# Moving one state product to another accumulator bank, and four steps of a hand-written schedule, in a fused state-space and feed-forward kernel

## The chip, the cores and the metric

The kernel runs on one NeuronCore of a Trainium2 chip. Five engines work side by side, each through its own queue in the order in which the program emits: TensorE (PE, with its weight loads shown as PEld), VectorE (DVE), ScalarE (ACT), GpSimd (POOL) and SyncE (SP), whose queue issues most DMAs here. The metric is the time of one execution on the device in microseconds. The kernel before takes 117.77 us, the median of six runs (117.53 to 119.92).

## The reference

Two stages follow each other. The first is a chunked state-space recurrence over batch 4, 8 heads, 768 positions, head size 32 and state size 16; the second is a feed-forward layer with a squared ReLU over 3072 rows, 256 wide, 2048 hidden:

```
for each chunk c of 32 positions:
    cum    = cumsum(log a)                       # in the chunk
    M      = (C B^T) * exp(cum_i - cum_j) * (i >= j)
    y      = M x + (C state) * exp(cum)
    state  = exp(sum log a) * state + sum_j B_j x_j exp(cum_last - cum_j)
x = y as rows of 3072 x 256
out = max(x w_in, 0)^2 w_out
```

The chunk length changes nothing in the result. The kernel uses longer stretches of its own.

## The kernel before

**Units and blocks.** The sequence is cut into 12 units, `UNITS[k] = (b, j)`: batch b and a third j of its positions, 256 rows, k = 4 j + b. A unit of the first stage becomes a block of 256 rows of the second. All is done in bf16 products with float32 accumulation.

**First stage of a unit k.** `ph_load` (line 124) brings B, C and x to the tiles `B_nat`, `C_nat`, `x_nat`. `prep_c` and `prep_b` (lines 161 and 169) multiply C and B with decay factors into `jt[k % 3]`, two instructions each; `prep_x` (line 180) casts x to `xs`. All three are POOL's from the third unit's C on, except some early ones. `ph_tr` (line 199) transposes jt to `bct`: for k < 5 with six PE transposes and a copy from PSUM by DVE (by ACT for k = 1), for later units with one DMA transpose on SP's queue. `ph_mt` (line 231) makes the scores, 16 products into four PSUM banks 0 to 3; `ph_mask` (line 253) multiplies one bank with the causal mask on DVE into `mts`, four times per unit. `ph_yu(y, u)` (line 260) makes the output products of unit y, first those from the incoming state (`from_state`, which read `Sd`), then, in the same call, the state products of unit u (`state_products`, two results U of 64 columns), then the products within the unit; ACT copies the outputs to `T`. `ph_s(k, i)` (line 333) turns U into the running state z (ACT's copy, or DVE's instruction of line 349) and then makes `Sd` on POOL (line 354), which the next output products read.

**Second stage.** For each of 8 steps f of a block: `mm1` (line 368), the up-projection, four 128x256 products into a PSUM bank, then ReLU by ACT to `hb`; `square` (line 380) on DVE; `mm2` (line 386), the down-projection, four products into bank 7 (bank 6 for block 0), which after the eighth step are copied by ACT and sent to memory by SP.

**Banks.** PSUM has 8 banks of 512 float32. 0 to 3 hold scores, 7 (or 6) the down-projection, and 4, 5 and 6 go round by `bank()`, least recently taken first; a bank that holds U is in `held` until `ph_s` has been emitted. `ph_s` reads U, so what overwrites that place waits for it.

**The order of the work.** It is written by hand; no planner moves anything. Blocks 0 and 1 follow the list `first` (line 539). From step 16 on, one up-projection is emitted in each step s, `ups[s]`; `at(s, fn, ...)` puts first-stage work ahead of it, in the order in which the `at` calls were made, then come the square of the step before and a down-projection. Step 22 has no down-projection; before it, `mm2(2, s - 19)`, after it, `mm2(*ups[s - 4])`. In step 19 the order for POOL is: `prep_x` of unit 4, then `Sd` of unit 3 twice (from `ph_s`), then `prep_c` and `prep_b` of unit 5. In SP's queue stand, in this order: the loads of units 3, 4 and 5, two output stores, the loads of unit 6, the transpose of unit 5, the loads of unit 7, the next store and the transpose of unit 6.

Of the kernel before, what the change touches and what calls it, by code (L numbers as in the profile page):

```python
# [16 lines left out]
def _fap(base: bass.AP, offset_elems: int, free_dims):  # L17

    ap0 = list(base.ap)[0]
    return bass.AP(tensor=base.tensor, offset=base.offset + offset_elems,  # L20
                   ap=[list(ap0)] + [list(d) for d in free_dims])
# [9 lines left out]
def kernel(  # L31
# [69 lines left out]
    held = set()  # L101

    def take(*hs):
        for h in hs:
            assert h not in held
            order.remove(h)
            order.append(h)

    def bank(edge=False):

        h = next(h for h in order if not (edge and h == 5))
        take(h)
        return h

    def two_banks():
        h = min(((4, 5), (5, 6)), key=lambda p: max(order.index(i) for i in p))
        take(*h)
        return h
# [80 lines left out]
    def ph_tr(k):  # L199
        v = live.setdefault(k, {})  # L200
        bct = big.tile([128, 2, 3, 128], BF16, tag="bct", name=f"bct{k}")
        v["bct"] = bct
        if k >= NPE:
            nc.sync.dma_start_transpose(out=bct.rearrange("p r w t -> p (r w) t"),
                                        in_=jt[k % 3].rearrange("p r w t -> p (r w t)"))
            return
        if k == 0:
            for r in range(2):
                tr = pp[:, 6 + r, 0:192].bitcast(BF16)
                for w in range(3):  # L210
                    nc.tensor.transpose(tr[:, w * 128:(w + 1) * 128], jt[0][:, r, w, :], eye_b)
                o = bct[:, r].rearrange("p w t -> p (w t)")
                if r == 0:
                    nc.vector.tensor_copy(out=o, in_=tr)
                else:
                    nc.scalar.copy(out=o, in_=tr)
            return
        tr = pp[:, {1: 7, 2: 1, 3: 2}.get(k) or bank(), 0:384].bitcast(BF16)
        for r in range(2):
            for w in range(3):  # L220
                o = (r * 3 + w) * 128
                nc.tensor.transpose(tr[:, o:o + 128], jt[k % 3][:, r, w, :], eye_b)  # L222
        o = bct.rearrange("p r w t -> p (r w t)")
        if k == 1:
            nc.scalar.copy(out=o, in_=tr)  # L225
        else:
            nc.vector.tensor_copy(out=o, in_=tr)
# [32 lines left out]
    def ph_yu(y=None, u=None, late=False, h=None, split=False, by_head=False):  # L260

        if h is None and u not in (0, 1, 3):
            h = two_banks()
        begun = set()

        def mm(hb, quads, dst, w, v, pos):
            need = [(hb, q) for q in quads if (hb, q) not in begun]
            begun.update(need)
            assert len(need) in (0, len(quads))
            nc.tensor.matmul(dst, w, v, start=bool(need), stop=False, skip_group_check=True,  # L270
                             **({} if pos is None else {"tile_position": pos}))

        def from_state():
            for i in range(2):
                S_i = live[y]["S"][i]
                if S_i is None:
                    continue
                for g in range(2):
                    mm(h[i], range(4), pp[:, h[i], g * 128:(g + 1) * 128], S_i[:, g * 128:(g + 1) * 128],
                       _fap(live[y]["bct"], 128 + g * 128 + i * 64, [[384, 2], [1, 64]]), None)  # L280

        def state_products():
            v, last = live[u], UNITS[u][1] == 2
            if u < 2:
                v["U"] = [(6, 0), (7, 384)]
            elif u == 3:
                v["U"] = [(bank(), 256), (7, 256)]
            else:
                v["U"] = [(h[i], 256) for i in range(2 - last)]
            held.update(x[0] for x in v["U"] if x[0] < 7)  # L290
            for r in range(2):
                for i in range(2 - last):
                    for q in range(4):
                        mm(v["U"][i][0], [q], pp[32 * q:32 * q + 32, v["U"][i][0], v["U"][i][1]:v["U"][i][1] + 64],
                           jt[u % 3][64 * i:64 * i + 64, r, 0, 32 * q:32 * q + 32],
                           _fap(v["xs"][64 * i:64 * i + 64], q * 64 + r * 32, [[256, 2], [1, 32]]),
                           (64 * i, 32 * q))

        def within(qs):
            v = live[y]  # L300
            for g in range(2):
                for r in range(2):
                    for i in range(2):
                        for q in qs:
                            hd = 4 * g + q
                            mm(h[i], [q], pp[32 * q:32 * q + 32, h[i], g * 128:(g + 1) * 128],
                               v["xs"][64 * i:64 * i + 64, hd, r * 32:r * 32 + 32],
                               v["mts"][64 * i:64 * i + 64, q, r, g, :], (64 * i, 32 * q))

        if y is not None and not late:  # L310
            from_state()
        if u is not None and not by_head:
            state_products()
        if y is not None:
            for qs in [[q] for q in range(4)] if by_head else [range(4)]:
                within(qs)
        if u is not None and by_head:
            state_products()
        if y is not None:
            if late:  # L320
                from_state()
            T[y] = tpool.tile([128, 2, 2, 2, 64], BF16, tag="T", name=f"T{y}")
            if y > 2:
                live.pop(y)
            if split:
                for i, fn in enumerate((nc.scalar.copy, nc.vector.tensor_copy)):
                    fn(out=_fap(T[y], i * 64, [[128, 4], [1, 64]]),
                       in_=_fap(pp, h[i] * 512, [[64, 4], [1, 64]]))
                return
            nc.scalar.copy(out=_fap(T[y], 0, [[64, 2], [128, 4], [1, 64]]),  # L330
                           in_=_fap(pp, h[0] * 512, [[(h[1] - h[0]) * 512, 2], [64, 4], [1, 64]]))
# [48 lines left out]
    def square(blk, fp):  # L380
        hb = hbs.pop((blk, fp))
        h2 = hpool.tile([128, 2, 256], BF16, tag="h2", name=f"h2{blk}_{fp}")
        nc.vector.tensor_tensor(out=h2, in0=hb, in1=hb, op=ALU.mult)  # L383
        h2s[(blk, fp)] = h2
# [24 lines left out]
    with tc.manual_schedule():  # L409
# [125 lines left out]
        for q in range(4):  # L535
# [3 lines left out]
        first = """  # L539
            u00 u01 s00 Y1 d00 s01 u10 z1b d01 u11 load s10 u02 s11 u03 d10 inv s02 u12 d11 s03 u13 d02 s12 d03 u04  # L540
            s13 d12 u05 B2 s04 d13 free tr2 u14 s05 u15 d04 s14 mt2 d05 m20 load3 s15 U2 m21 d14 m22 prep3 d15 u06 m23
            u16 lend s06 u07 Y2 s16 d06 u17 s07 d16 d07 s17""".split()
        for what in first:
            if what in phases:
                phases[what]()
# [10 lines left out]
        ups = [(b, f) for b in range(NU) for f in range(8)]  # L556
        todo = {}

        def at(s, fn, *args, **kw):
            todo.setdefault(s, []).append((fn, args, kw))  # L560
# [4 lines left out]
        at(18, ph_mt, 3)  # L565
        at(18, ph_mask, 3, 0)
        at(19, prep_x, 4, nc.gpsimd)
        at(19, ph_yu, u=3)
        at(26, ph_s, 2, 1, raw=U21)
        for k in range(2, NU):  # L570
            s0 = {2: 16, 3: 22}.get(k, 8 * k - 4)
            if k == NU - 1:
                at(s0, ph_yu, y=k)
                break
            if k > 2:
                at(s0, ph_yu, y=k, u=k + 1)
                at(s0, ph_mt, k + 1)
            for i in range(2):
                at(s0 + (3 if k == 2 else 1), ph_s, k + 1, i)
            for q in range(k == 2, 4):  # L580
                at(s0 + {2: (None, 3, 4, 5), 3: (1, 2, 3, 4)}.get(k, (1, 2, 4, 6))[q], ph_mask, k + 1, q)
        at(20, ph_tr, 4)
# [2 lines left out]
        at(22, ph_tr, 5)  # L585
        at(23, prep_x, 5, nc.gpsimd)
        for k in range(6, NU):
            at(max(17, 8 * k - 33), ph_load, k)
            at({6: 25}.get(k, 8 * k - 25), ph_prep, k)
            at(8 * k - 20, ph_tr, k)  # L590
        for s in range(16, len(ups) + LAG):
            for fn, args, kw in todo.pop(s, []):
                fn(*args, **kw)
            if s < len(ups):
                mm1(*ups[s], any(fn is ph_yu for fn, _, _ in todo.get(s + 1, [])))
            if 17 <= s <= len(ups):
                square(*ups[s - 1])
            if s == 16:
                mm2(1, 7)
            elif 19 <= s < 22:  # L600
                mm2(2, s - 19)
            elif s > 22:
                mm2(*ups[s - LAG])
# [1 line left out]
_INS = ['x', 'a', 'B', 'C', 'moe_w_in', 'moe_w_out']  # L605
# [26 lines left out]
```

## Time and profile before

| | before |
|---|---|
| median of six runs | 117.77 us (117.53 to 119.92) |
| the profiled execution | 117.54 us |
| its span | 115.8 us |
| PE busy | 109.1 us, 94% |
| DVE busy | 82.1 us, 71% |
| ACT busy | 73.7 us, 64% |
| POOL busy | 50.5 us, 44% |
| mean granted TensorE clock | 0.998 |

The span runs from the first to the last instruction of the program in one profiled execution; the execution's own time has 1.7 us more around it. A busy share is an average over the span. PE's matmuls overlap each other, so the start of one group against the start of the next tells more than its busy time. All positions below are microseconds from the span's start. In the lines of a timeline the columns are start, length, engine, source line, operation, what it writes and reads, and, in brackets, the idle time ahead of it with what ended it.

### The profile page before, as it was taken

How to read it: one execution, taken by the hardware profiler on the slowest of the kernel's cores; microseconds unless marked ns; L12 is line 12 of the kernel's file. 1: busy time of each engine (PE TensorE's matmuls, PEld its weight loads, DVE VectorE, ACT ScalarE, POOL GpSimd, SP SyncE). 2: the span in 40 equal slices, each digit the busy share in tenths (PEclk: the TensorE clock that was granted, in tenths of full speed). 3: DMA queues.
4: the chain of work that ended last, by engine and by line, in shares of the span. 5: the costliest groups of instructions: out<-in, count | busy, mean ns of one | idle time of the engine just before them, and what ended most of it. 6: DMA issues, size and time to landing. Idle time of an engine off the chain costs nothing.

```text
span 115.8 us, 4019 instructions
## 1 busy us (share of the span) xinstructions
PE 109.1 (94%) x1650; PEld 91.7 (79%) x1650; DVE 82.1 (71%) x184; ACT 73.7 (64%) x135; POOL 50.5 (44%) x102
## 2 busy tenths in 40 slices
PE   6998999999889989999999999999999999999980
PEld 6976688777566878888888888888888888888860
DVE  4498868796498999848949868767777578355440
ACT  3345575536745775776676776776767766966830
POOL 7489998133698978408409229037020020000000
PEclk9999999999999999999999999999999999999999
DMA  3999999948999999916918628541060020010202
GB/s 70 205 174 127 184 129 175 190 61 153 185 187 225 196 95 223 198 36 170 171 34 181 132 90 145 113 127 38 0 158 6 3 93 8 18 72 0 91 5 91
DMA packets 46387, 13.20 MB, mean 114 GB/s; under 512 B 41376, under 2 KB 44896, under 8 KB 46368
## 3 DMA queue, kind: packets, MB, share of 16 engines
q1 hardware_dynamic: 40736, 10.13, 46.1%
q0 software_dynamic: 4336, 2.49, 16.6%
q10 hardware_dynamic: 1296, 0.32, 1.2%
q8 instruction: 13, 0.21, 0.9%
q14 instruction: 6, 0.05, 0.2%
HBM read 10.64 MB, written 3.15 MB: 119 GB/s over the span
## 4 chain that ended last, share of the span: by engine, by line
PE 75%; DMA 10%; POOL 7%; ACT 2%; DVE 2%; issue 2%; POOLq 0%; DVEq 0%
PE pp L393 32%; PE pp L373 30%; DMA B_nat<-in_B_dram 5%; PE pp L270 5%; DMA bct<-jt 4%; PE pp L159 4%; PE pp L237 3%; POOL Sd L354 2%; POOL w_in_b L150 1%; PE pp L222 1%; POOL C_nat L135 1%; POOL w_out_b L154 1%; POOL jt L177 1%; POOL jt L164 1%; DVE jt L177 1%
## 5 line engine op out<-in xcount | busy, mean ns | idle before, releaser
L377 ACT ACTIVATE hb<-pp 128x512 bf16<-128x512 f32 x96 | 56.7, 597 | 28.6 <-PE pp L373 26.6
L373 PE MATMUL pp<-T,w_in_b 128*128 128x256 bf16 x384 | 56.8, 273 | 0.5 <-ACT T L330 0.3
L393 PE MATMUL pp<-w_out_b,h 128*128 128x256 bf16 x384 | 56.5, 273 | 0.4 <-DVE z L349 0.4
L383 DVE TENSOR_TENSOR h<-hb 128x512 bf16<-128x512 bf16 x96 | 43.3, 460 | 17.1 <-ACT hb L377 17.0
L373 PEld LDWEIGHTS <-w_in_b 128*128 128x128 bf16 x384 | 36.4, 98 | 7.1 <-issue 2.4
L393 PEld LDWEIGHTS <-h 128*128 128x128 bf16 x384 | 37.0, 98 | 5.7 <-issue 0.6
L255 DVE TENSOR_TENSOR mts<-pp,mask 128x512 bf16<-128x512 f32 x46 | 31.0, 682 | 1.0 <-PE pp L237 1.0
L354 POOL TENSOR_TENSOR Sd<-z,QP 128x256 bf16<-128x256 f32 x20 | 12.7, 648 | 32.7 <-DVE z L349 32.7
L164 POOL TENSOR_TENSOR jt<-C_nat,P_sb 128x128 bf16<-128x128 f32 x22 | 10.1, 478 | 3.3 <-DMA C_nat<-in_C_dram 3.3
L177 POOL TENSOR_TENSOR jt<-B_nat,Pinv 128x128 bf16<-128x128 f32 x18 | 9.1, 523 | 0.3 <-PE pp L393 0.3
L159 PE MATMUL pp<-idle 128*128 128x128 bf16 x72 | 7.0, 273 | 1.1 <-DVE idle L422 1.1
L349 DVE SCALAR_TENSOR_TENSOR z<-z,Ptot,pp 128x64 f32<-128x64 f32 x14 | 3.9, 280 | 5.6 <-ACT T L330 4.6
L189 POOL CAST xs<-x_nat 128x512 bf16<-128x512 f32 x10 | 6.8, 685 | 0.7 <-DMA x_nat<-in_x_dram 0.7
L159 PEld LDWEIGHTS <-idle 128*128 128x128 bf16 x72 | 6.3, 129 | 1.1 <-DVE idle L422 1.1
L406 ACT COPY osb<-pp 128x512 f32<-128x512 f32 x11 | 6.4, 582 | 0.4 <-PE pp L393 0.4
L330 ACT CAST T<-pp 128x512 bf16<-128x512 f32 x10 | 5.9, 585 | 1.1 <-PE pp L270 0.6
L237 PE MATMUL pp<-bct 32*64 32x256 bf16 x192 | 5.1, 280 | 1.0 <-DMA bct<-jt 0.3
L270 PE MATMUL pp<-mts,xs 64*32 64x128 bf16 x352 | 5.5, 219 | 0.0
L270 PEld LDWEIGHTS <-xs 64*32 64x32 bf16 x352 | 3.7, 90 | 0.8 <-issue 0.4
L270 PE MATMUL pp<-bct,Sd 128*128 128x128 bf16 x40 | 4.2, 220 | 0.0
L237 PEld LDWEIGHTS <-bct 32*64 32x64 bf16 x192 | 2.0, 102 | 2.4 <-ACT bct L225 0.5
L270 PEld LDWEIGHTS <-Sd 128*128 128x128 bf16 x40 | 3.1, 98 | 0.4
(65 smaller groups left out, 43.5 us busy)
## 6 DMA issues: line engine op xcount, KB each, us to landing
x_nat<-in_x_dram SPq DMA_DIRECT2D x11, 256.0 KB, 4.6
out_dram<-osb SPq DMA_DIRECT2D x11, 256.0 KB, 2.2
C_nat<-in_C_dram SPq DMA_DIRECT2D x11, 128.0 KB, 3.6
B_nat<-in_B_dram SPq DMA_DIRECT2D x9, 128.0 KB, 4.2
w_in_b<-in_moe_w_in_dram POOLq DMA_DIRECT2D x4, 256.0 KB, 6.1
w_out_b<-in_moe_w_out_dram POOLq DMA_DIRECT2D x4, 256.0 KB, 5.7
B_nat<-in_B_dram ACTq DMA_DIRECT2D x1, 128.0 KB, 3.2
C_nat<-in_C_dram POOLq DMA_DIRECT2D x1, 128.0 KB, 6.6
```

The lines of the kernel that those rows point to most:

```text
L159: nc.tensor.matmul(pp[:, 5, 0:128], idle, idle, start=True, stop=True, skip_group_check=True)
L164: eng.tensor_tensor(out=_fap(jt[k % 3], 128 + 144 * g, [[384, 2], [32, 4], [1, 16]]), in0=_fap(loaded[k]["C"], 128 * g, [[16, 2], [32, 4], ...
L177: eng.tensor_tensor(out=o, in0=i, in1=_fap(Pinv, b * 24 + 12 * g + j, [[96, 2], [3, 4], [0, 16]]), op=ALU.mult)
L189: eng.tensor_copy(out=xs, in_=loaded[k]["x"])
L237: nc.tensor.matmul(pp[64 * u:64 * u + 64, q, r * 256:r * 256 + 256], bct[32 * q:32 * q + 32, r, 0, u * 64:u * 64 + 64], _fap(bct[32 * q:32 ...
L255: nc.vector.tensor_tensor(out=live[k]["mts"][:, q], in0=(pp[:, q, :] if t is None else t).rearrange("p (r g i) -> p r g i", r=2, g=2), in1 ...
L270: nc.tensor.matmul(dst, w, v, start=bool(need), stop=False, skip_group_check=True, **({} if pos is None else {"tile_position": pos}))
L354: nc.gpsimd.tensor_tensor(out=_fap(S_d, 0, [[128, 2], [32, 4], [1, 32]]), in0=_fap(z, 0, [[32, 2], [0, 4], [1, 32]]), in1=_fap(QP, ((b * 3 ...
L373: nc.tensor.matmul(pp[:, h, i * 256:(i + 1) * 256], w_in_b[wb][:, g, (wo + i) * 128:(wo + i + 1) * 128], T[blk][:, g].rearrange("p r u t - ...
L377: nc.scalar.activation(out=hb.rearrange("p i t -> p (i t)"), in_=pp[:, h, :], func=AF.Relu)
L383: nc.vector.tensor_tensor(out=h2, in0=hb, in1=hb, op=ALU.mult)
L393: nc.tensor.matmul(o, h2[:, i, r * 128:(r + 1) * 128], w_out_b[wb][:, wo + i, :], start=(f == 0 and (end or r == 0)), stop=(f == 15), skip ...
```

## The change

Seven places of the schedule are edited.

- The transposes of unit 4 (`ph_tr`, k = 4) are copied from PSUM by ACT instead of DVE.
- The second state product of unit 3 goes to bank 0, columns 256 to 319, instead of the same columns of bank 7. Bank 0 is one of the score banks and is not put into `held`.
- In the first list, the square of (1, 6) is emitted ahead of the output products of unit 2 (`Y2`) instead of behind them.
- The state products of unit 3 and both `ph_s` of unit 3 are emitted in step 20 instead of 19. What else is emitted in step 19 (`prep_x` of unit 4, mask (3, 1), `prep_c` and `prep_b` of unit 5) stays.
- The loads of unit 6 move from step 17 to 22, where they are emitted after the transpose of unit 5; those of unit 7 from 23 to 27.
- The preparation of unit 6 moves from step 25 to 28, that of unit 7 from 31 to 33, and the transpose of unit 6 from step 28 to 31.
- The step without a down-projection is 26 instead of 22; in between, the down-projection is three steps behind its up-projection instead of four.

```diff
@@ ph_tr
-        if k == 1:
+        if k in (1, 4):
             nc.scalar.copy(out=o, in_=tr)
@@ ph_yu, state_products
             elif u == 3:
-                v["U"] = [(bank(), 256), (7, 256)]
+                v["U"] = [(bank(), 256), (0, 256)]
             else:
                 v["U"] = [(h[i], 256) for i in range(2 - last)]
-            held.update(x[0] for x in v["U"] if x[0] < 7)
+            held.update(x[0] for x in v["U"] if 3 < x[0] < 7)
@@ first
-            u16 lend s06 u07 Y2 s16 d06 u17 s07 d16 d07 s17""".split()
+            u16 lend s06 u07 s16 Y2 d06 u17 s07 d16 d07 s17""".split()
@@ steps
-        at(19, ph_yu, u=3)
+        at(20, ph_yu, u=3)
         at(26, ph_s, 2, 1, raw=U21)
...
             for i in range(2):
-                at(s0 + (3 if k == 2 else 1), ph_s, k + 1, i)
+                at(s0 + (4 if k == 2 else 1), ph_s, k + 1, i)
...
         for k in range(6, NU):
-            at(max(17, 8 * k - 33), ph_load, k)
-            at({6: 25}.get(k, 8 * k - 25), ph_prep, k)
-            at(8 * k - 20, ph_tr, k)
+            at({6: 22, 7: 27}.get(k, 8 * k - 33), ph_load, k)
+            at({6: 28, 7: 33}.get(k, 8 * k - 25), ph_prep, k)
+            at({6: 31}.get(k, 8 * k - 20), ph_tr, k)
...
-            elif 19 <= s < 22:
-                mm2(2, s - 19)
-            elif s > 22:
+            elif 19 <= s < 26:
+                mm2(*ups[s - 3])
+            elif s > 26:
                 mm2(*ups[s - LAG])
```

## The prediction

> **What bounds the kernel now.** I read the page's first and fourth parts, then the timeline of TensorE (PE), then those of GpSimd (POOL) and SyncE's DMA queue (SP) over the stretch that the change touches, and last the single instructions there.
>
> ```profile
> PE 109.1 (94%) x1650; PEld 91.7 (79%) x1650; DVE 82.1 (71%) x184; ACT 73.7 (64%) x135; POOL 50.5 (44%) x102
> PE 75%; DMA 10%; POOL 7%; ACT 2%; DVE 2%; issue 2%; POOLq 0%; DVEq 0%
> ```
>
> PE is the bound, and the chain that ended last lies on it for 75%. From 43.6 us on, PE's groups of four 256-column products follow each other every 0.437 us and nothing waits until the last output copy. Only holes before that point can be closed. PE's timeline shows them (columns: start, length, instruction, idle time and what ended it):
>
> ```profile
> 29.97 0.51 PE L222 MATMUL pp<-eye_b,jt 128*128 128x128 bf16 x6
> 30.31 0.60 PE L373 MATMUL pp<-T,w_in_b 128*128 128x256 bf16 x4
> 31.13 0.42 PE L237 MATMUL pp<-bct 32*64 32x256 bf16 x16 [0.21 <-DVE bct L227]
> ...
> 32.21 0.61 PE L373 MATMUL pp<-T,w_in_b 128*128 128x256 bf16 x4
> 33.20 0.60 PE L393 MATMUL pp<-w_out_b,h 128*128 128x256 bf16 x4 [0.38 <-DVE z L349]
> ...
> 35.71 0.28 PE L270 MATMUL pp<-bct,Sd 128*128 128x128 bf16 x2
> ...
> 36.85 0.61 PE L373 MATMUL pp<-T,w_in_b 128*128 128x256 bf16 x4
> 37.67 0.60 PE L373 MATMUL pp<-T,w_in_b 128*128 128x256 bf16 x4 [0.21 <-DVE z L349]
> ...
> 42.42 0.51 PE L270 MATMUL pp<-mts,xs 64*32 64x128 bf16 x32
> 43.28 0.42 PE L237 MATMUL pp<-bct 32*64 32x256 bf16 x16 [0.35 <-DMA bct<-jt]
> ```
>
> A stall is the distance between two starts less 0.44 us for the work of the first group. **Down-projection (2,0)** at 33.20: 0.99 - 0.44 = 0.55, because its bank 7 still holds the fourth unit's second state product until VectorE (DVE) has made z from it. **Up-projection (2,7)** at 37.67: 0.82 - 0.44 = 0.38, because its bank waits for z of the fifth unit. **Scores of unit 5** at 43.28: 0.86 - 0.44 = 0.42, for the DMA transpose. Inside unit 3's output products another 0.08 is lost to the last mask, which DVE writes from 35.43 to 36.11. The scores of unit 3 at 31.13 lose 0.38 to DVE's copy of the transposes.
>
> **The change, part by part.**
>
> *Square before Y2.* Down-projection (1,6) starts 27.94, 0.62 after its predecessor, so 0.18 late; its square now fits into DVE's idle 0.49 us before 27.12 (activation ready about 26.65, square 0.41). But down-projection (1,7) depends on up-projection (1,7) at 27.31 (ends 27.92), ScalarE (ACT) 28.00 to 28.60, DVE 28.63 to 29.13, and stays at 29.26. Behind it the transposes of unit 3 wait for POOL until 29.91 anyway. Gain 0; if the square did not fit, the half copy of T would be 0.4 later, at 27.9, still before its reader at 28.82.
>
> *Bank 0 for the second product, one step later.* Down-projection (2,0) no longer waits: -0.55. Bank 0 is free then: mask (3,0) ends 32.29, and the products come near 32.8. The next scores need bank 0 back; z would be read by 33.9, far ahead of them.
>
> *Fifth transposes copied by ACT.* DVE loses a copy of 0.54 (34.63 to 35.17); ACT gains one of 0.80 (its only row of this shape, line 225, 798 ns). Activation (2,4) then ends near 35.0, with its reader after that idle. DVE's sequence from 31.60 on, without the copy and without the wait for z at 32.86, ends the last mask at about 35.4: -0.08.
>
> *Step without down-projection from 22 to 26.* Eleven groups lie between the scores of unit 4 and the products of unit 4 in both versions. Down-projection (2,3) now fills the 0.38 hole. At step 26 two up-projections follow each other; ACT needs 0.60 for each and PE 0.44, so ACT falls 0.16 behind, which three banks carry: 0.
>
> *Seventh unit's loads.* Three DMAs leave SP's queue ahead of transpose (5):
>
> ```profile
> 35.31 0.65 SPq L135 DMA_DIRECT2D C_nat<-in_C_dram  x1
> 36.06 0.66 SPq L135 DMA_DIRECT2D B_nat<-in_B_dram  x1
> 36.77 1.30 SPq L135 DMA_DIRECT2D x_nat<-in_x_dram  x1
> 38.25 1.32 SPq L204 DMA_TRANSPOSE bct<-jt  x1
> ```
>
> That transpose took 5.0 us to land, 43.23. It will be issued when POOL has unit 5's jt, near 36.4, and even 5 us end at 41.4: -0.42. The three loads follow near 37.7 and land some 4 us later; unit 6's jt is then made about 42.7 to 44.6 behind the Sd of step 26, its transpose issued near 44.7 lands near 48.7 (4.0 us before), wanted at 51.8. POOL's Sd of unit 5 come behind that preparation, near 46.4, and are wanted at 51.0. The eighth unit's three loads move too, and have more room. All hidden; 3 us is the cover.
>
> Removed so far: 0.55 + 0.38 + 0.42 + 0.08 = 1.43.
>
> *What is put behind what on POOL.* This decides. Step 19 still emits prep_c and prep_b of unit 5; ph_s of unit 3, formerly ahead of them in step 19, now comes in step 20, behind them. Before:
>
> ```profile
> 33.22 0.61 POOL L189 CAST xs<-x_nat 128x512 bf16<-128x512 f32 x1 [0.26 <-DMA x_nat<-in_x_dram]
> 33.79 1.36 POOL L354 TENSOR_TENSOR Sd<-z,QP 128x256 bf16<-128x256 f32 x2
> 35.11 1.03 POOL L164 TENSOR_TENSOR jt<-C_nat,P_sb 128x128 bf16<-128x128 f32 x2
> 36.10 1.15 POOL L177 TENSOR_TENSOR jt<-B_nat,Pinv 128x128 bf16<-128x128 f32 x2
> ```
>
> Unit 3's outputs (35.71) begin with two products from Sd, and PE waits there with all that follows. After the change POOL does four jt instructions first. Their inputs are late themselves: C of unit 5, issued at 29.82, took 4.3 us (34.08 with the exact length), and POOL starts some 0.13 after a landing: 34.22. B (30.62 + 4.3 = 34.91) is there in time for the third.
>
> How long the four take: three such instructions at 31.26 to 32.4 took 403, 408 and 412 ns (pitch 0.37) beside masks; at 36.10 two took 586 and 602 (pitch 0.56) beside DVE's squares. Three squares fall into 34.2 to 36.3. By the rows: 34.22 + 0.37 + 3 x 0.56 = 36.27; Sd 0.61 (608 is the least of seven), 36.88; to PE 0.06 (POOL's jt ends 29.91, PE starts 29.97): **36.94**. A rule of the Trainium skill is harsher: "SBUF - State Buffer", section "Who interferes with whom", says that VectorE's tensor_tensor with both inputs in SBUF, as a square has, takes the read port that GpSimd uses, and the second to come waits for the whole of the first. Three squares of 0.41 would add 1.23 instead of 3 x 0.19: 34.22 + 4 x 0.37 + 1.23 + 0.67 = **37.60**. The trace shows 0.19 per meeting, and I take the rows. The lower bound is four at 0.37: 34.22 + 0.74, third at 35.04 when B lands, 35.78, Sd and PE: 36.45. With loads 0.4 us earlier POOL would start at 33.83, and PE at 36.0.
>
> Without POOL, PE would reach this point at 31.13 + 0.36 (scores) + 7 x 0.437 + 0.10 + 0.18 (state products) + 0.35 (transposes) = 35.18. So a new stall of 36.94 - 35.18 = **1.76** takes the place of those removed. From there to the scores of unit 5: 0.21 + 0.07 + 0.44 + 0.36 + 11 x 0.437 + 0.01 + 0.82 = 6.70, at 43.64 against 43.28 before: **+0.36**. Thus the span of 115.8 becomes about 116.1, the profiled execution's 117.54 about 117.9. It is 0.23 below the median of six; I add the difference to the median: 117.77 + 0.36 = 118.13, rounded 118.1.
>
> A second rule weighs on this gap. "TensorE: Matmul & The Clock Gate", section "What's actually happening", has the clock halve after an idle window of about 3.4 us. The granted clock here is 1.00 in every stretch from 26.8 on, with holes up to 0.55. A gap of 1.76 is half the window, so by the row and by the rule I add 0; were the gate to close for one window, half of 3.4, 1.7 us, would be lost.
>
> **Rivals.** (a) *Port lock in full* or a longer chain on POOL: 37.60, +1.02, **118.8**. For it: one Sd of 790 ns stands at 33.79 beside a square. Against: 0.19 is the usual meeting. (b) *POOL not slowed*, or loads earlier: 36.45 to 36.0, -0.13 to -0.58, **117.2 to 117.6**. For it: POOL's ops beside masks take 0.41, and landings can vary. Against: POOL and DVE both have work throughout. (c) *The other side: Sd not late at all*, because unit 5's jt does not hold POOL up: PE goes on at 35.18, reaches the scores of unit 5 at 41.88 and gains 1.40, **116.4**. The whole of it needs Sd's end before 35.1; more than 0.3% is gained once it ends before 36.17. Against it: C lands only at 34.08. (d) *Clock gate closes* over the gap: +2.06, **119.8**. Against: no drop in this trace.
>
> **How the numbers follow.** 0.3% (0.35 us) is about what a measurement of this kernel can tell from no change. The likeliest case, 0.55, has its own range 117.8 to 118.4; its middle lies on that bound, so 0.28 slower and 0.27 same. (a) 0.20, slower. (b) 0.13: 0.08 same, 0.05 faster. (c) 0.07, faster. (d) 0.05, slower. Sums: faster 0.12, same 0.35, slower 0.53. The range runs from (b)'s lower end to just above (a), 117.2 to 118.9, and leaves out (c) and (d).
>
> **What would show it.** Right: PE's two products from Sd at 36.5 to 37.2 with over 1 us of idle time ended by POOL Sd; POOL's Sd of unit 3 behind four jt; no wait at down-projection (2,0), at up-projection (2,7) or at the scores of unit 5; transpose (5) issued ahead of C of unit 6, near 36.4. Wrong: Sd ahead of jt, or PE through the output products by 36; a new wait after 43.6, of scores for a transpose or of outputs for Sd, would mean that the 3 us of cover were not there; a granted clock under 1.

## The result and the profile after

The changed kernel takes 118.19 us (median of 35 runs, 117.14 to 121.40) against 117.78 (72 runs, 116.75 to 121.53) for the kernel before. The ratio is 1.0027 with a 95% interval of 1.0008 to 1.0046: a loss of 0.3 us. A second comparison gave 117.84 against 117.72, ratio 1.0004 (0.9977 to 1.0031), and shows no loss. Both lie within 0.3%. The change removes four waits and puts a fifth of about their size in their place.

The profiled execution of the changed kernel has one of the disturbances that the comparison leaves out, a stretch of half clock. I therefore read two profiles: this one, and one of another execution of the same kernel (`e0_after`), whose span is 115.6 us. First PE's timeline in the second, to be laid beside the ten lines of before (columns as there):

```profile
31.26 1.05 PE L373 MATMUL pp<-T,w_in_b 128*128 128x256 bf16 x8
32.14 0.60 PE L393 MATMUL pp<-w_out_b,h 128*128 128x256 bf16 x4
...
34.51 0.60 PE L393 MATMUL pp<-w_out_b,h 128*128 128x256 bf16 x4
36.32 0.28 PE L270 MATMUL pp<-bct,Sd 128*128 128x128 bf16 x2 [1.21 <-POOL Sd L354]
...
37.84 0.60 PE L393 MATMUL pp<-w_out_b,h 128*128 128x256 bf16 x4
38.33 0.60 PE L373 MATMUL pp<-T,w_in_b 128*128 128x256 bf16 x4
...
42.64 0.51 PE L270 MATMUL pp<-mts,xs 64*32 64x128 bf16 x32
43.07 0.42 PE L237 MATMUL pp<-bct 32*64 32x256 bf16 x16
```

Down-projection (2,0) at 32.14 follows its two up-projections (31.26 + 2 x 0.44) without the old 0.55, up-projection (2,7) at 38.33 with 0.05 instead of 0.38, the scores of unit 5 at 43.07 with nothing instead of 0.42. In their place stands 36.32 - 34.51 - 0.44 = 1.37 us ahead of unit 3's output products, ended by POOL's Sd. From the transposes of unit 3 (29.75 here, 29.97 before) to the scores of unit 5 pass 13.32 us, before 13.31. From there to the end of ACT's last output copy both take 69.62. The waits were exchanged one for the other.

POOL's timeline of the first profile and then of the second shows the cause. Both have four jt instructions of unit 5, lines 164 and 177, ahead of Sd. (The idle 0.37 in the second is put down to PE; C of unit 5 had landed at 33.66, 0.14 ahead of the first jt, and nothing of PE that touches this jt is so late.)

```profile
34.26 0.89 POOL L189 CAST xs<-x_nat 128x512 bf16<-128x512 f32 x1 [0.24 <-DMA x_nat<-in_x_dram]
35.22 0.97 POOL L164 TENSOR_TENSOR jt<-C_nat,P_sb 128x128 bf16<-128x128 f32 x2
36.16 0.97 POOL L177 TENSOR_TENSOR jt<-B_nat,Pinv 128x128 bf16<-128x128 f32 x2
37.09 1.36 POOL L354 TENSOR_TENSOR Sd<-z,QP 128x256 bf16<-128x256 f32 x2
```

```profile
33.80 0.78 POOL L164 TENSOR_TENSOR jt<-C_nat,P_sb 128x128 bf16<-128x128 f32 x2 [0.37 <-PE pp L373]
34.57 0.93 POOL L177 TENSOR_TENSOR jt<-B_nat,Pinv 128x128 bf16<-128x128 f32 x2
35.46 1.56 POOL L354 TENSOR_TENSOR Sd<-z,QP 128x256 bf16<-128x256 f32 x2
```

The first profile has the longer wait, 37.94 - 35.73 - 0.44 = 1.77 us, and something more behind it. Its PE timeline, and its busy times by stretch (the eighth column, after the five engines, is the granted clock):

```profile
35.73 0.60 PE L393 MATMUL pp<-w_out_b,h 128*128 128x256 bf16 x4
37.94 0.28 PE L270 MATMUL pp<-bct,Sd 128*128 128x128 bf16 x2 [1.61 <-POOL Sd L354]
...
40.26 1.06 PE L373 MATMUL pp<-T,w_in_b 128*128 128x256 bf16 x4
41.12 1.06 PE L393 MATMUL pp<-w_out_b,h 128*128 128x256 bf16 x4
41.97 1.06 PE L373 MATMUL pp<-T,w_in_b 128*128 128x256 bf16 x4
...
43.31 0.60 PE L373 MATMUL pp<-T,w_in_b 128*128 128x256 bf16 x4
```

```profile
36.00:39.50 3.50, 1.89 (x75) 1.18 (x73) 1.41 (x3) 1.10 (x2) 2.45 (x5) 1.00 0.76 189
39.50:42.90 3.40, 3.40 (x19) 2.42 (x17) 3.15 (x7) 1.21 (x3) 1.93 (x3) 0.50 0.78 143
42.90:50.00 7.10, 7.10 (x124) 6.10 (x123) 5.49 (x14) 5.13 (x9) 5.55 (x11) 1.00 0.77 159
```

Groups that otherwise follow each other every 0.437 us come every 0.85 us for 3.4 us: the clock was halved from 39.5 to 42.9, 1.6 us after PE had resumed. The five groups from 39.46 to 43.31 took 3.85 us instead of 2.19, so this cost 1.67.

### The profile page after: what moved, and what is told of

It reads as the page before. It is cut to its first block, busy times and chain, and to the rows that moved or that the text cites. A ratio compares the mean times of both kernels' runs of the same rounds, so it can differ in the third digit from the quotient of the medians.

```text
span 118.8 us, 4017 instructions
## 1 busy us (share of the span) xinstructions
PE 110.1 (93%) x1650; PEld 92.4 (78%) x1650; DVE 82.6 (70%) x183; ACT 74.4 (63%) x136; POOL 51.0 (43%) x102
## 2 busy tenths in 40 slices
DMA packets 46387, 13.20 MB, mean 111 GB/s; under 512 B 41376, under 2 KB 44896, under 8 KB 46368
## 4 chain that ended last, share of the span: by engine, by line
PE 80%; DVE 4%; DMA 4%; ACT 4%; POOL 3%; issue 1%; SPq 1%; ACTq 0%
PE pp L373 33%; PE pp L393 33%; PE pp L270 7%; DMA x_nat<-in_x_dram 4%; PE pp L237 4%; PE pp L159 3%; DVE h L383 2%; ACT hb L377 1%; SPq L135 1%; POOL jt L177 1%; POOL xs L189 1%; DVE Pinv L530 1%; PE pp L222 1%; ACT bct L225 1%; POOL Sd L354 1%
## 5 line engine op out<-in xcount | busy, mean ns | idle before, releaser
L393 PE MATMUL pp<-w_out_b,h 128*128 128x256 bf16 x384 | 57.6, 276 | 1.3 <-DVE h L383 1.1
L383 DVE TENSOR_TENSOR h<-hb 128x512 bf16<-128x512 bf16 x96 | 44.1, 466 | 18.7 <-ACT hb L377 18.4
L373 PEld LDWEIGHTS <-w_in_b 128*128 128x128 bf16 x384 | 37.1, 99 | 6.8 <-issue 2.3
L164 POOL TENSOR_TENSOR jt<-C_nat,P_sb 128x128 bf16<-128x128 f32 x22 | 10.6, 503 | 2.4 <-PE pp L270 2.0
```

What stands on the lines that cost most here:

```text
L164: eng.tensor_tensor(out=_fap(jt[k % 3], 128 + 144 * g, [[384, 2], [32, 4], [1, 16]]), in0=_fap(loaded[k]["C"], 128 * g, [[16, 2], [32, 4], ...
L373: nc.tensor.matmul(pp[:, h, i * 256:(i + 1) * 256], w_in_b[wb][:, g, (wo + i) * 128:(wo + i + 1) * 128], T[blk][:, g].rearrange("p r u t - ...
L393: nc.tensor.matmul(o, h2[:, i, r * 128:(r + 1) * 128], w_out_b[wb][:, wo + i, :], start=(f == 0 and (end or r == 0)), stop=(f == 15), skip ...
```

## The experiments

All ratios are against runs of the kernel before made beside them, with 95% intervals. "Distance" is the time from the start of unit 3's transposes to the start of unit 5's scores in the profile: 13.31 before. It leaves out what happens ahead of unit 3's transposes, which moves by up to 1 us from one execution to the next, and so it leaves out the swap of square and `Y2` too. It is one execution's number, and the ratio comes from many. "To the end" is from there to the end of the last output copy, 69.62 before.

**The changed kernel again** (`e0_after`), no edit.

> The changed kernel once more, for a trace without a drop of the clock and beside the runs of the same chip. Theory S (Sd of unit 3 queued behind unit 5's jt on POOL eats what the other edits save): PE waits 1.5 to 2.0 us ahead of unit 3's output products, ended by POOL Sd, and from unit 3's transposes to unit 5's scores pass 13.5 to 13.8 us (13.31 before); time +0.2 to +0.5 us on before. Theory C (the clock gate is what makes the change slower): the wait is there too, but in executions without a drop the time is below before, and a drop to half clock of about 3.4 us follows the wait in most of them.

Measured: 117.84 us, ratio 1.0004 (0.9977 to 1.0031), distance 13.32, wait 1.37. All three are below what theory S expected (+0.2 to +0.5 us, 13.5 to 13.8, 1.5 to 2.0): C of unit 5 landed 3.9 us after the start of the transposes instead of 4.2. The wait itself, ended by POOL's Sd, is there as expected. Theory C as a whole falls, since without a drop the time is not below before.

**Unit 5's jt behind unit 3's Sd** (`e1_sd_first`, and again as `e1_again`), one line's place on POOL:

```diff
-        at(19, prep_c, 5, nc.gpsimd)
-        at(19, prep_b, 5, nc.gpsimd)
+        at(20, prep_c, 5, nc.gpsimd)
+        at(20, prep_b, 5, nc.gpsimd)
```

> The changed kernel with one step mended: prep_c and prep_b of unit 5 emitted in step 20, behind unit 3's Sd, as POOL had them before the change. Theory S: PE reaches unit 3's output products near 5.2 us after unit 3's transposes and doesn't wait; jt of unit 5 ends near 37.3, its transpose lands near 41.3, in time for scores at 41.9; from transposes to scores 11.9 us, time 1.4 us below before, 116.4 (up to 116.8 if the transpose takes 5 us). Theory C: without the long wait no drop, and the time also falls, but only in the executions that had one. Rival (loads or a bank make it slower): as the changed kernel, 118.1.

> e1_sd_first once more, beside the runs of this call that differ from it by one edit: 116.7, 12.5 us from unit 3's transposes to unit 5's scores.

Measured: 116.67 us, ratio 0.9930 (0.9907 to 0.9954), and 116.33 us, ratio 0.9900 (0.9866 to 0.9935); distances 12.47 and 12.14. The output products of unit 3 began 5.20 after the transposes (35.18 - 29.97 = 5.21 in the prediction) and no wait for Sd is left. The gain is 0.8 to 1.2 us, not the whole 1.4. PE's timeline of the first of the two shows why:

```profile
35.09 0.28 PE L270 MATMUL pp<-bct,Sd 128*128 128x128 bf16 x2
35.30 0.25 PE L270 MATMUL pp<-xs,jt 64*32 64x64 bf16 x16
35.37 0.22 PE L270 MATMUL pp<-mts,xs 64*32 64x128 bf16 x3
36.04 0.41 PE L270 MATMUL pp<-mts,xs 64*32 64x128 bf16 x29 [0.45 <-DVE mts L255]
```

Three products within the unit run, the fourth waits for the fourth mask. DVE ended it 6.09 after the transposes, because two squares ahead of it took 861 and 609 ns beside POOL's instructions instead of 0.41. In the two profiles of the changed kernel the fourth mask ended 5.6 and 5.7 after the transposes, hidden under the wait for Sd. The mask's share differs from one execution to the next: in the second profile of this kernel the squares took less and it cost 0.2, not 0.6.

**Only POOL's new order, in the kernel before** (`e2_sd_late_only`):

```diff
+        at(19, prep_c, 5, nc.gpsimd)
+        at(19, prep_b, 5, nc.gpsimd)
         at(19, ph_yu, u=3)
...
-        at(19, prep_c, 5, nc.gpsimd)
-        at(19, prep_b, 5, nc.gpsimd)
```

> The kernel before with only the one new order on POOL: prep_c and prep_b of unit 5 ahead of unit 3's Sd. Theory S: output products of unit 3 wait until 36.9 instead of 35.7, the wait of 0.38 for z of the fifth unit stays, the wait of 0.42 for the transpose goes: scores of unit 5 at 44.0 against 43.3, time +0.7, 118.5. Rival (POOL's order costs nothing): 117.8.

Measured: 117.85 us, ratio 1.0023 (0.9997 to 1.0050): 0.3 us at most likely, between nothing and 0.6, where 0.7 was expected. The products began 6.28 after the transposes, not 7.0, as C had landed at 3.6; from there 6.70 and the 0.36 for z give the measured distance of 13.34. The order alone costs 0.5 in PE's wait (6.28 against 5.75), of which the transpose wait of before pays the 0.42 and the mask's the 0.08. In the profile the wait for Sd is there, so the mechanism holds; the expected size does not, and in time a loss is not clear of zero. The wait follows the landing of C.

**The moved loads undone, on top of e1** (`e3_sd_first_loads_back`):

```diff
-            at({6: 22, 7: 27}.get(k, 8 * k - 33), ph_load, k)
-            at({6: 28, 7: 33}.get(k, 8 * k - 25), ph_prep, k)
-            at({6: 31}.get(k, 8 * k - 20), ph_tr, k)
+            at(max(17, 8 * k - 33), ph_load, k)
+            at({6: 25}.get(k, 8 * k - 25), ph_prep, k)
+            at(8 * k - 20, ph_tr, k)
```

> As e1_sd_first, but the loads, preparations and the transpose of units 6 and 7 in the steps that they had before. Theory S, with the loads in SP's queue ahead of the transpose of unit 5: that transpose lands near 43.2 as before, and PE, earlier by 1.4, waits for it: scores at 43.3, time as before, 117.8. So the moved loads would be worth 1.4 here, and not the 0.42 that the trace of before shows. Rival (the moved loads are worth their 0.42 only): 116.8.

Measured: 117.36 us, ratio 0.9961 (0.9932 to 0.9990), distance 13.56. The profile shows the wait:

```profile
42.05 0.51 PE L270 MATMUL pp<-mts,xs 64*32 64x128 bf16 x32
44.00 0.42 PE L237 MATMUL pp<-bct 32*64 32x256 bf16 x16 [1.45 <-DMA bct<-jt]
```

In this execution theory S holds to the letter (landing 13.5 after the transposes). But this execution took 118.32 us against the median of 117.36. By the ratios the moved loads are worth 0.4 us (0.9961 against 0.9930; the intervals overlap), so the landing is not always so late: in the profiles of `e2_sd_late_only` and `e4_bank_only`, with the loads in the same place, the transpose of unit 5 landed 11.2 and 11.6 after those of unit 3.

**Bank 0 alone** (`e4_bank_only`):

```diff
-                v["U"] = [(bank(), 256), (7, 256)]
+                v["U"] = [(bank(), 256), (0, 256)]
...
-            held.update(x[0] for x in v["U"] if x[0] < 7)
+            held.update(x[0] for x in v["U"] if 3 < x[0] < 7)
```

> The kernel before with bank 0 for unit 3's second state product and nothing else. Theory (two chains meet at unit 5's scores): the wait of 0.55 at down-projection (2,0) goes, but the last mask still ends 6.1 after unit 3's transposes and holds the output products, and behind them the transpose of unit 5 lands 13.3 after, as SP's queue still has unit 6's loads ahead of it: PE's gain turns into a longer wait there, time 117.7. Rival (the bank alone is worth its stall): 117.2.

Measured: 118.14 us, ratio 1.0024 (0.9991 to 1.0057), distance 13.13. No gain, and the rival's 117.2 is ruled out. Of the two expected reasons the first is in the profile: the mask takes 0.5 more inside the output products than before. The second is not in this execution, where the transpose landed in time. A third was not foreseen. The state products want bank 0 while DVE still reads it for mask (3,0); first before, then here:

```profile
32.02 0.25 PE L270 MATMUL pp<-xs,jt 64*32 64x64 bf16 x16
```

```profile
32.07 0.69 DVE L255 TENSOR_TENSOR mts<-pp,mask 128x512 bf16<-128x512 f32 x1
32.50 0.56 PE L270 MATMUL pp<-xs,jt 64*32 64x64 bf16 x16
```

The sixteen products take 0.31 longer: the fifth, the first into bank 0, starts 0.05 after the mask's end at 32.76. So bank 0 in step 19 gains 0.25 of the 0.55, and the output products start 5.50 after the transposes instead of 5.75. In step 20 this wait is gone (two profiles of the changed kernel), which is what moving the products a step down is good for; its price was paid on POOL. Why the mean is no better than before, with a distance 0.18 shorter, stays open; a loss isn't shown either.

**The products back in step 19** (`e6_products_step19`):

```diff
-        at(20, ph_yu, u=3)
+        at(19, ph_yu, u=3)
...
-                at(s0 + (4 if k == 2 else 1), ph_s, k + 1, i)
+                at(s0 + (3 if k == 2 else 1), ph_s, k + 1, i)
```

> The changed kernel with one edit undone: state products and both ph_s of unit 3 in step 19 again, so that their Sd stand ahead of unit 5's jt on POOL; bank 0 and all else as changed. Theory S: no wait for Sd, output products of unit 3 near 5.2 after its transposes, held up inside by the last mask as in the run that moved the jt (0.5); 12.5 from transposes to scores, 116.7. Rival (the step of the products itself, and not the order on POOL, is what counts): something else than the run that moved the jt.

Measured: 116.64 us, ratio 0.9908 (0.9873 to 0.9943), distance 12.55. The time and the distance are as expected, the way there is not quite: the output products began 5.50 after the transposes and not 5.2, because the state products waited 0.3 for mask (3,0) as in `e4_bank_only`, and the last mask cost 0.3 and not 0.5. No wait for Sd is left. As in e1, undoing one edit of seven gives a gain of 0.9% on before; what the two kernels have in common, against the changed one, is POOL's order, which they reach in different ways.

**Squares of (2,2) to (2,5) on ACT** (`e7_squares_act`):

```diff
-        nc.vector.tensor_tensor(out=h2, in0=hb, in1=hb, op=ALU.mult)
+        if blk == 2 and 2 <= fp < 6:
+            nc.scalar.activation(out=h2, in_=hb, func=AF.Square)
+        else:
+            nc.vector.tensor_tensor(out=h2, in0=hb, in1=hb, op=ALU.mult)
```

> The changed kernel with the squares of (2,2) to (2,5) computed by ScalarE instead of VectorE, so that no instruction of VectorE with two SBUF inputs runs beside unit 5's jt on POOL. Theory P (squares lengthen POOL's instructions by 0.19 each): all four jt take about 0.41 (pitch 0.37), Sd 0.61; from the first jt to Sd's start 1.5 instead of 1.7 to 1.9, PE's wait 0.2 to 0.5 shorter, time 117.4 to 117.6. Rival (POOL's lengths have another cause): jt of 0.6 and an Sd of 0.8 remain, time as the changed kernel, 117.8.

Measured: 117.46 us, ratio 0.9974 (0.9948 to 0.9999), distance 13.20. The tile view of jt on POOL, first in this kernel, then in the first profile of the changed kernel (lengths in ns: least, median, most):

```profile
L164 POOL TENSOR_TENSOR jt<-C_nat,P_sb x2: 411/412/412, 34.0 to 34.4; 128x128 bf16<-128x128 f32 x2
L177 POOL TENSOR_TENSOR jt<-B_nat,Pinv x2: 410/410/410, 35.0 to 35.4; 128x128 bf16<-128x128 f32 x2
```

```profile
L164 POOL TENSOR_TENSOR jt<-C_nat,P_sb x2: 408/508/607, 35.2 to 35.6; 128x128 bf16<-128x128 f32 x2
L177 POOL TENSOR_TENSOR jt<-B_nat,Pinv x2: 403/502/602, 36.2 to 36.5; 128x128 bf16<-128x128 f32 x2
```

Without squares all four take 0.41 and Sd 613 ns; with them two take 0.60 and Sd 790. That DVE's squares lengthen POOL's work is shown in this pair of profiles. The output products began 6.48 after the transposes, against 7.02 and 6.57 in the two profiles of the changed kernel; the gain is no larger because the third jt now waits for B: it starts at 35.03, after a gap of 0.27 ended by that load. What the shorter instructions are worth in time stays open: the ratio's interval is clear of the changed kernel's 1.0027 (1.0008 to 1.0046), but not of its 1.0004 (0.9977 to 1.0031), and neither was measured beside this run.

**The last mask one square earlier** (`e8_mask_early`), on top of e1:

```diff
-                at(s0 + {2: (None, 3, 4, 5), ...
+                at(s0 + {2: (None, 3, 4, 4), ...
```

> As e1_sd_first (unit 5's jt behind unit 3's Sd), and the last mask of unit 3 emitted in step 20, ahead of the square of (2,3). Theory: with Sd no longer late, the mask was next (0.57 inside the output products); one square of 0.4 to 0.6 earlier on VectorE it costs 0.1 or nothing: 11.9 to 12.05 from unit 3's transposes to unit 5's scores, time 116.2. Rival (what is next is the transpose of unit 5, which landed 10.2 after): no gain beyond e1, 116.7.

Measured: 116.86 us, ratio 0.9914 (0.9879 to 0.9948), distance 11.90: the whole 1.41, and the mask no longer shows among PE's waits. The time, however, is no better than e1's: from unit 5's scores to the end pass 70.16 instead of 69.62; unit 6's scores wait:

```profile
49.43 0.51 PE L270 MATMUL pp<-mts,xs 64*32 64x128 bf16 x32
50.41 0.42 PE L237 MATMUL pp<-bct 32*64 32x256 bf16 x16 [0.47 <-DMA bct<-jt]
```

**Unit 7's loads behind that transpose** (`e9_loads7_later`), on top of e8:

```diff
-            at({6: 22, 7: 27}.get(k, 8 * k - 33), ph_load, k)
+            at({6: 22, 7: 31}.get(k, 8 * k - 33), ph_load, k)
```

> As e8_mask_early, with the loads of unit 7 in step 31, behind the transpose of unit 6 in SP's queue. In e8 that transpose was issued 44.9 and landed 50.4, behind unit 7's loads, and unit 6's scores waited 0.54 for it. Theory (its landing waits for the bytes ahead of it in the queue): it lands near 48, no wait, 11.9 from unit 3's transposes to unit 5's scores and 69.6 from there to the end, time 1.4 below before, 116.3. Rival (preparation, not the queue, makes it late): the wait of 0.5 stays.

Measured: 115.79 us, ratio 0.9864 (0.9833 to 0.9894), distance 11.90 and 69.62 to the end. SP's queue in e8, then here:

```profile
40.75 1.94 SPq L135 DMA_DIRECT2D C_nat<-in_C_dram  x1
42.74 0.58 SPq L135 DMA_DIRECT2D B_nat<-in_B_dram  x1
43.36 0.75 SPq L135 DMA_DIRECT2D x_nat<-in_x_dram  x1
44.21 0.55 SPq L407 DMA_DIRECT2D out_dram<-osb  x1
44.94 1.25 SPq L204 DMA_TRANSPOSE bct<-jt  x1
```

```profile
41.51 0.36 SPq L407 DMA_DIRECT2D out_dram<-osb  x1
43.39 1.24 SPq L204 DMA_TRANSPOSE bct<-jt  x1
44.67 0.58 SPq L135 DMA_DIRECT2D C_nat<-in_C_dram  x1
```

With three loads less ahead of it the transpose landed 2.8 us after its issue instead of 5.4. It was also issued 1.3 us earlier, counted from unit 3's transposes, because C of unit 6 landed 1.0 earlier and POOL made the jt sooner. Either would have covered the wait of 0.54, so the queue and the preparation are not told apart; both follow from moving unit 7's loads. PE waits for nothing between unit 3's scores and the end. This is the fastest kernel of the case, 1.4% below before, in six executions; its interval still overlaps those of e1 and e8, so it is the profile, and not the time alone, that shows what the last mend did.

**Fifth transposes on DVE** (`e5_copy_dve`), on top of e1:

```diff
-        if k in (1, 4):
+        if k == 1:
```

> As e1_sd_first, with the fifth transposes copied by VectorE again. Theory: the last mask holds unit 3's output products in e1, and VectorE now has 0.54 more ahead of it: 13.0 from transposes to scores, 117.2. Rival (the copy is hidden on either engine, as the zero gain that the recorded sum gives it beyond 0.08 would have it): as e1.

Measured: 116.71 us, ratio 0.9931 (0.9892 to 0.9970), distance 12.56 with a mask wait of 0.5, against 0.9900 and 12.14 for e1 measured beside it. The copy on DVE lies ahead of the mask as the theory has it, but the intervals overlap, and the other profile of e1 has 12.47: squares that meet POOL's instructions move the mask as much as the copy does. Inconclusive.

**The swap of square and Y2 undone** (`e10_swap_undone`), on top of e1:

```diff
-            u16 lend s06 u07 s16 Y2 d06 u17 s07 d16 d07 s17""".split()
+            u16 lend s06 u07 Y2 s16 d06 u17 s07 d16 d07 s17""".split()
```

> As e1_sd_first, with the square of (1,6) behind unit 2's output products again, as before the change. Theory (0, because unit 3's transposes wait for B of unit 3 on POOL anyway): time as e1, 116.7; down-projection (1,6) 0.2 later than in e1, unit 3's transposes no later. Rival (the swap is worth its 0.18): 116.9.

Measured: 116.96 us, ratio 0.9934 (0.9909 to 0.9959) against 0.9900 (0.9866 to 0.9935) for e1; distance 12.10, and 69.83 to the end. The intervals overlap, so time leaves open whether the swap is worth nothing or up to about 0.4. Down-projection (1,6) is 0.18 later than in e1, counted from unit 2's output products, as expected. From these products to unit 3's transposes pass 3.56 us here, and 3.71, 3.76 and 3.72 in the other profiles with the old order (before, e2, e4). In the ten profiles with the new order it is 3.31 to 3.57, with a median of 3.50. That speaks for the rival's 0.18, though this run against e1 (3.50 and 3.55) shows less.

## Why the prediction was right, and where it was not

**The time.** 118.13 was forecast (+0.36), 118.19 measured (ratio 1.0027, +0.32). The likeliest case is the one that happened: waits of 1.43 removed, a wait for Sd put in. The forecast lay on the bound of 0.3% and leaned towards slower; measured, it is the near side of that bound, and the second comparison (+0.05) shows no loss at all. That the number came out within 0.1 us is partly luck. The wait for Sd alone differs by 0.4 between two executions of the changed kernel, which is as much as the whole forecast. And two terms named below, the landing of C and the swap, were each off by some 0.2 in the same direction; an estimate with both mended comes out near 0, at the second comparison and not at the first.

**The removed waits.** All four went. What they are worth shows only with Sd out of the way: 0.8 to 1.2 us below before in e1 and e6, more than half of 1.43, and 1.6 in e9, which has two further mends.

**The new wait.** 1.76 was predicted, 1.77 and 1.37 were seen. The first profile agrees even inside: first jt at 4.30 after unit 3's transposes (4.25 predicted), Sd's end 2.66 later (2.66 predicted). Three squares met POOL there as counted, only the third met Sd and not a jt, at the same price of 0.19. The harsher reading, that the second to come waits for the whole of the first, would have given 1.23 for three; the trace has about 0.57. The second profile is 0.4 shorter, mostly because C landed 0.3 earlier. That landing was a fixed 34.08 in the sum, and against PE it moves between executions, from 3.6 to 4.2 after unit 3's transposes in the fourteen profiles. The load itself does not: from issue to landing it took 4.1 to 4.4 us in all of them. What moves is its issue, 0.1 to 0.7 ahead of the transposes. e2, with C at 3.6, missed by 0.4 for the same reason.

**From there to the scores.** 6.70 predicted (its parts as written add up to 6.72), 6.75 in the second profile.

**The wait of 0.42 for the transpose** was taken from one execution. e2 and e4 have it not at all and e3 has 1.45, so its size is that of one execution. The ratios of e3 and e1 put its mean near 0.4, with intervals that overlap.

**The mask, 0.08.** The last mask was put at 5.4 after the transposes (35.4), with squares of 0.41. It ended at 5.6 and 5.7 in the changed kernel and at 6.09 in e1, where squares beside POOL take up to 0.86. In the changed kernel this is covered by the wait for Sd, so it did not show in the result; with POOL's order mended (e1 twice, e3, e6, e10) it took 0.1 to 0.6.

**"Gain 0" for the swap.** Its reason, that unit 3's transposes wait for POOL anyway, held in the first profile of the changed kernel, as it did before. It failed in the second, where they start at 29.75 with no wait behind the down-projection at 29.30, and in the eleven profiles of the other runs. The worth is likelier near 0.2 than 0 (e10).

**The cover of 3 us for the moved loads** held: in the first profile the transpose of unit 6 landed at 49.9 and its scores came at 54.5; in the second, without the drop of the clock, 47.4 and 51.25. In e8 it is eaten up: PE is 1.4 us earlier, and the transpose lands 2.9 us later after unit 3's transposes than in the second profile.

**"By the row and by the rule I add 0" for the clock gate** failed for some executions: in the first profile the drop came behind the wait of 1.77, half of the idle window that the rule asks for, and it cost the 1.7 that rival (d) names. The mean granted clock was below 0.99 in 8 of 59 executions of the changed kernel, in 4 of the 153 of the kernel before that have a clock on record, and in 2 of the 111 of the kernels with Sd in time (e1 twice, e3, e5, e6, e8, e9, e10). At 1.67 us each, 8 in 59 against 4 in 153 would be some 0.2 us on the mean, an estimate from these counts. That the long wait brings the drop is likely by these counts and not shown: `e7_squares_act`, with a wait of about 1.3 us, has none in 22, and no run varied the wait alone.

## What to carry to other kernels

When a step is moved in a schedule that several engines share, write down each engine's queue before and after: here the state products went one step down for PE's sake, and on POOL their successors slipped behind four instructions whose own inputs were late. What a queue's first instruction waits for (a landing) sets everything behind it, so put short work that the critical engine needs ahead of work that waits for a load. And after each mend look for the next wait: Sd, then the mask, then a transpose behind loads in a queue held the gain in turn, and only with the third mend does the profile show the whole of it. Ask also when a shared place becomes free: bank 0 cost 0.3 us in the step where a mask still read it (e4, e6), and the step later, where that is gone, is what put Sd back.

## What the runs showed of the hardware

In the first profile a wait of 1.77 us on TensorE was followed by 3.41 us at half clock, which began 1.6 us after the products had resumed and cost 1.67 us. The 3.41 us ahead of the drop (36.1 to 39.5) held nothing but this wait, 1.1 us of products on small tiles, and 0.5 us of full ones. In the second a wait of 1.37 us was not followed by a drop. The Trainium skill, "TensorE: Matmul & The Clock Gate", section "What's actually happening", has windows of this length that run freely, not from the kernel's start; that would fit a drop in some executions only, but no run here varied it.

A VectorE product of two SBUF operands and a GpSimd instruction that reads SBUF lengthen each other when they overlap, one of them or both: GpSimd's by about 0.2 us (0.41 becomes 0.56 to 0.66, 0.61 becomes 0.77 to 0.81), VectorE's from 0.41 to as much as 0.86. In the first profile two of the three squares that met POOL kept 0.41. With the squares moved to ScalarE all of GpSimd's were at their shorter length.

A DMA transpose of the same size landed 2.8 us after its issue with one store directly ahead of it in the queue (e9), and 5.4 behind three loads and that store (e8). Loads ahead do not always delay it so; how far they still are from landing goes with it. Of the 28 transposes of units 5 and 6 in the fourteen profiles, twelve were issued when the last load ahead landed at most 1.0 us later, and took 2.8 to 3.0 us. For the other sixteen that load landed 1.2 to 3.9 us after the issue, and they took 3.0 to 5.8. Within that range the runs show no rule.
